# One VectorE maximum over four score banks in place of four maxima, in a fused attention and SwiGLU kernel

## The chip, the cores and the metric

The kernel runs on one core of one Trainium2 chip. The metric is the device time of one execution in microseconds, as the median of several runs.

## The reference

Eight batches of eight heads attend over 576 positions with a head width of 64. Scores that lie more than `tau` under the largest of their row are dropped before the softmax. The result is laid out as 4608 tokens of 512 features and goes through a SwiGLU block of width 1536. Everything is float32.

```python
scores = scale * np.matmul(q, k.transpose(0, 1, 3, 2))          # (8, 8, 576, 576), scale = 1/8
thresh = np.max(scores, axis=-1, keepdims=True) - tau
scores = np.where(scores >= thresh, scores, -1000000000.0)
scores = scores - np.max(scores, axis=-1, keepdims=True)
attn = np.exp(scores)
attn = attn / (np.sum(attn, axis=-1, keepdims=True) + 1e-09)
attn_out = np.matmul(attn, v)
x = attn_out.transpose(0, 2, 1, 3).reshape(4608, 512)
g = x @ w_gate
out = (g / (1 + np.exp(-g)) * (x @ w_val)) @ w_out
```

## The kernel before

A unit of attention work is a pair of heads of one batch, so there are 32 pairs. The program has three stages.

**Early tiles (7 to 130 us).** The four pairs of the first batch go through `scores()`, 20 query tiles in all. A tile of 128 rows puts the scores of its two heads into two PSUM tiles `sc` of two banks each; the last 64 rows of a pair need one such tile. VectorE takes one maximum per PSUM tile (L455), ScalarE the exponentials (L459), VectorE masks and sums them (L462).

**Main slots (130 to 1143 us).** The other 28 pairs take three slots each, 84 in all, and twelve slots make up one batch. `slot_scores` (L1705) runs 32 small score products (64 PE instructions) into two PSUM tiles, one per head, of two banks. Bank 0 and bank 1 of a head hold 288 columns each of units u=0 and u=1, and behind them 144 columns each of unit u=2. Then `slot_rest` lists the work on the other engines:

- four maxima on VectorE, two for each head: units 0 and 1 in one instruction (L1726), unit 2 in the other (L1728). They write six columns of `mx`, negated;
- a query row's keys lie in two groups of 32 partitions, so the six values are exchanged between neighbouring groups, by VectorE (`largest`, four instructions, L1734) or by ScalarE (`others`, four copies, L1740), and one small reduce joins own and other value into `nm` (L1735 or L1744);
- ScalarE makes the threshold `th` from `nm` (L1747);
- for each of the six (head, unit) blocks ScalarE writes the exponential of the scores (L1751, "E" in what follows), and VectorE multiplies it by the comparison of the scores with the threshold and sums (L1753, "M"). Both read the scores in PSUM;
- ScalarE exchanges the sums (L1761), VectorE adds them and takes the reciprocal (L1766, L1767), ScalarE or POOL scale the blocks (L1779, L1776), VectorE transposes them (L1781). `attend` (L1802) multiplies with the values one pair later.

Between the score products of one slot and the next, TensorE runs products of the SwiGLU block (`block_part`; L993, L1473, L1482, L1269).

**Tail (1143 us on).** The SwiGLU products of the last tokens. `more_banks` hands the score banks to them.

The order on each engine is made by a planner, `Plan`, as the program is written: `job(engine, cost, fn, *deps)` enters a step with an assumed cost, and the planner issues steps by their due times and ranks. TensorE's order is fixed by the code; `slot_scores` waits in the plan for all six M of the slot before (`sc_users`).

What really waits for what on the chip are semaphore waits that the tile framework adds. For a PSUM tile it keeps accesses of different engines in the order in which they were issued, over the whole tile and reads included. In the built program of before, the third E of a slot (head 0, unit 1, bank 1) so waits for the first M of the slot (head 0, unit 0, bank 0), and the first M of head 1 waits only for the first E of head 1, which is in the other tile.

Of the kernel before, what the change touches and what calls it, by code (L numbers as in the profile page):

```python
# [10 lines left out]
F32 = mybir.dt.float32  # L11
# [3 lines left out]
ALU = mybir.AluOpType  # L15
AX = mybir.AxisListType
# [11 lines left out]
class Plan:  # L28
# [12 lines left out]
    def job(self, eng, took, fn, *deps, rank=1, lag=0.0, moves=0.0):  # L41
        j = Job(eng, took, fn, rank, lag, moves)
        for d in deps:
            if isinstance(d, Job) and d.end is None:
                d.then.append(j)
                j.waits += 1
            elif d is not None:
                j.ready = max(j.ready, self.after(d, eng) if isinstance(d, Job) else d + self.HOP)
        if not j.waits:
            self.open[eng].append(j)  # L50
        return j
# [61 lines left out]
def kernel(  # L113
# [11 lines left out]
    nc = tc.nc  # L125
    P = 128
# [5 lines left out]
    G = 32  # L132
# [7 lines left out]
    SH = S // 2  # L140
    NU3 = 3
    SQ = SH // 2
# [10 lines left out]
    const = ctx.enter_context(tc.tile_pool(name="const", bufs=1))  # L153
    qkp = ctx.enter_context(tc.tile_pool(name="qkp", bufs=2))
    stp = ctx.enter_context(tc.tile_pool(name="stp", bufs=4))
    ps_s = ctx.enter_context(tc.tile_pool(name="ps_s", bufs=2, space=bass.MemoryType.PSUM))
    ps_f = ctx.enter_context(tc.tile_pool(name="ps_f", bufs=1, space=bass.MemoryType.PSUM))
    hbm = ctx.enter_context(tc.tile_pool(name="hbm", bufs=1, space=bass.MemoryType.DRAM))
    ctx.enter_context(tc.manual_schedule())
# [6 lines left out]
    sums = deque(const.tile([P, 2 * NU3, 3], F32, name=f"sums{i}") for i in range(4))  # L166
    for x in sums:
        nc.vector.memset(x[:, :, 2], 1e-9)
    minus2 = const.tile([P, 1], F32, name="minus2")
    nc.vector.memset(minus2, -2.0)  # L170
    junk = const.tile([P, 1], F32, name="junk")
# [249 lines left out]
    heads = [slice(h * D, (h + 1) * D) for h in range(2)]  # L421
# [2 lines left out]
        return TA <= t < NT  # L424

    def statistics(*names):
        return [stp.tile([P, 2 * NU3, 2] if x == "mx" else [P, 2 * NU3], F32, name=x) for x in names]

    def scores(seg, t):
        qT, kT = seg["qT"], seg["kT"]  # L430
        q0 = t * P - seg["q0"]
        if t < NT:
            pss = [ps_s.tile([P, 2, 512], F32, name="sc") for _ in range(2)]
            for h, hs in enumerate(heads):
                cut_ = D if turned(t) and h == 1 else 0
                for n, lo, to in [(0, 0, D), (0, D, SH), (1, 0, SH)] if cut_ else [(0, 0, SH), (1, 0, SH)]:
                    at_ = (n * SH + lo - cut_) % S
                    nc.tensor.matmul(pss[h][:, n, lo:to], qT[hs, q0:q0 + P], kT[hs, at_:at_ + to - lo],
                                     start=True, stop=True)
        else:  # L440
            pss = [ps_s.tile([P, 2, 512], F32, name="sc")]
            for n, h in ((0, 0), (1, 1), (1, 0), (0, 1)):
                hs = heads[h]
                nc.tensor.matmul(pss[0][hs, n, 0:SH], qT[hs, q0:q0 + D], kT[hs, n * SH:(n + 1) * SH],
                                 start=True, stop=True)
        nm, th, ri, tot = statistics("nm", "th", "ri", "tot")
        sm = sums[0]
        sums.rotate(1)
        m = len(pss)
        scs = [ps[:, :, 0:SH] for ps in pss]  # L450
        both = pbufs[0].rearrange("p h s -> p (h s)")[:, KM:KM + P]
        ps = [pbufs[0][:, x, :].rearrange("p (n s) -> p n s", n=2) for x in range(m)]
        pbufs.rotate(1)
        for x in range(m):
            nc.vector.tensor_reduce(out=nm[:, x:x + 1], in_=scs[x], axis=AX.XY, op=ALU.max, negate=True)  # L455
        yield
        for x in range(m):
            nc.scalar.activation(th[:, x:x + 1], nm[:, x:x + 1], AF.Identity, bias=cut, scale=-1.0)
            nc.scalar.activation(ps[x], scs[x], AF.Exp, bias=nm[:, x:x + 1])  # L459
        yield  # L460
        for x in range(m):
            nc.vector.scalar_tensor_tensor(out=ps[x], in0=scs[x], scalar=th[:, x:x + 1], in1=ps[x],  # L462
                                           op0=ALU.is_ge, op1=ALU.mult, accum_out=sm[:, x, 0:1])
        nc.vector.tensor_reduce(out=tot[:, 0:m], in_=sm[:, 0:m, 0:3:2], axis=AX.X, op=ALU.add)
        nc.vector.reciprocal(out=ri[:, 0:m], in_=tot[:, 0:m])
        units = [ident] * m
        if t >= TA:
            for x in range(m):
                if x % 2:
                    nc.gpsimd.tensor_scalar(out=ps[x], in0=ps[x], scalar1=ri[:, x:x + 1], scalar2=None, op0=ALU.mult)  # L470
                else:
                    nc.scalar.activation(ps[x], ps[x], AF.Copy, scale=ri[:, x:x + 1])
        yield
        if t < TA:
            units = [dbufs[0][:, x, :] for x in range(m)]
            dbufs.rotate(1)
            for x in range(m):
                nc.scalar.activation(units[x], ident, AF.Copy, scale=ri[:, x:x + 1])
        unflipped.append((seg, t, both, [(p.rearrange("p n s -> p (n s)"), unit) for p, unit in zip(ps, units)]))
        yield  # L480
# [297 lines left out]
    job, pe = plan.job, plan.pe  # L778
# [113 lines left out]
    stores, summed_g, parts = {}, {}, []  # L892
# [796 lines left out]
    def slot_scores(seg, t):  # L1689


        plan.force(*seg["qk"])
        qT, kT = seg["qT"], seg["kT"]
        deps, sc_users[:] = sc_users[:], []
        pss = []

        def fn():
            pss.extend(ps_s.tile([P, 2, 512], F32, name="sc") for _ in heads)
            for u, part, keys in ((0, (0, slice(0, SH)), (0, SH)), (1, (1, slice(0, SH)), (0, SH)),
                                  (2, (0, slice(SH, SH + SQ)), (0, SQ)), (2, (1, slice(SH, SH + SQ)), (SQ, SH))):  # L1700
                for g in range(NG):
                    a, c = divmod(g, 2)
                    for h, hs in enumerate(heads):
                        col = (NU3 * t + u) * D + a * G
                        nc.tensor.matmul(pss[h][(slice(g * G, (g + 1) * G), *part)], qT[hs, col:col + G],  # L1705
                                         kT[hs, c * SH + keys[0]:c * SH + keys[1]], start=True, stop=True)

        return pss, pe(1.85, fn, *deps, *seg["qk"])

    def slot_rest(seg, t, pss, mark, pooled, max_by_act, rank):  # L1710
        m = 2 * NU3
        mx, nm, th, ri, tot = statistics("mx", "nm", "th", "ri", "tot")
        sm = sums[0]
        sums.rotate(1)
        old_sums, sum_users[0] = sum_users[0], []
# [4 lines left out]
        flat = {x: pall[:, at_of(*x):at_of(*x) + SH] for x in tiles}  # L1720
        ps = {x: y if x[1] < 2 else y.rearrange("p (a n) -> p a n", a=2) for x, y in flat.items()}
        n_of = lambda h, u: NU3 * h + u
        rs = []
        for h, tile_ in enumerate(pss):
            n = n_of(h, 0)
            rs.append(job("DVE", 0.72, lambda n=n, tile_=tile_: nc.vector.tensor_reduce(  # L1726
                out=mx[:, n:n + 2, 0], in_=tile_[:, :, 0:SH], axis=AX.X, op=ALU.max, negate=True), mark, rank=0))
            rs.append(job("DVE", 0.42, lambda n=n, tile_=tile_: nc.vector.tensor_reduce(  # L1728
                out=mx[:, n + 2:n + 3, 0], in_=tile_[:, :, SH:SH + SQ], axis=AX.XY, op=ALU.max, negate=True), mark, rank=0))

        def largest():
            for g in range(NG):
                o = g ^ 1
                nc.vector.tensor_reduce(out=mx[g * G:(g + 1) * G, 0:m, 1], in_=mx[o * G:(o + 1) * G, 0:m, 0:1], axis=AX.X, op=ALU.max)  # L1734
            nc.vector.tensor_reduce(out=nm[:, 0:m], in_=mx[:, 0:m, :], axis=AX.X, op=ALU.min)  # L1735

        def others():
            for g in range(NG):
                o = g ^ 1
                nc.scalar.copy(mx[g * G:(g + 1) * G, 0:m, 1], mx[o * G:(o + 1) * G, 0:m, 0])  # L1740

        if max_by_act:
            oj = job("ACT", 0.78, others, *rs, rank=0)
            nj = job("DVE", 0.18, lambda: nc.vector.tensor_reduce(out=nm[:, 0:m], in_=mx[:, 0:m, :], axis=AX.X, op=ALU.min), oj, rank=0)  # L1744
        else:
            nj = job("DVE", 0.82, largest, *rs, rank=0)
        ej = job("ACT", 0.25, lambda: nc.scalar.activation(th[:, 0:m], nm[:, 0:m], AF.Identity, bias=cut, scale=-1.0), nj, rank=0)  # L1747
        masks = {}
        for h, u in tiles:
            x, n = (h, u), n_of(h, u)  # L1750
# [20 lines left out]
        for u in range(NU3):  # L1771
            scaled = []
            for h in range(2):
                x, n = flat[h, u], n_of(h, u)
# [179 lines left out]
    for s, (n, x) in enumerate((n, x) for n in range(len(halved)) for x in range(NU3)):  # L1954
        seg = halved[n]
        i, t = seg["i"], seg["tiles"][x]
# [43 lines left out]
    def more_banks():  # L2000
        plan.force(*sc_users)
        for _ in range(2):
            ps = ps_s.tile([P, 2, 512], F32, name="sc")
            for h in range(2):
                b_ = Bank(None, ps[:, h])
                banks.append(b_)
# [57 lines left out]
```

## Time and profile before

| | |
|---|---|
| median of 3 runs | 1373.08 us (1371.66 to 1374.05) |
| profiled execution, first to last instruction (span) | 1369.2 us |
| TensorE matmul busy | 1351.0 us, 99% |
| VectorE busy | 1070.9 us, 78% |
| ScalarE busy | 875.5 us, 64% |
| granted TensorE clock | 1.000 |
| the four maxima of the slots, L1726 and L1728 | 124.8 us and 74.8 us, 168 instructions each |

The profiled execution has no other time of its own than its span of 1369.2 us. It is 3.9 us under the median of the runs; these 3.9 us lie around the instructions and are carried along unchanged. Mean durations are of instructions that may overlap by some hundredths of a microsecond with their neighbours on the same engine.

### The profile page before, as it was taken

The numbers are of one execution on the slowest core, as the hardware profiler recorded it, in microseconds if no ns is written. First come the engines' busy times: TensorE is split into PE (matmuls) and PEld (weight loads), VectorE is DVE, ScalarE is ACT, GpSimd is POOL, SyncE is SP. The second block draws the span as 40 slices with busy tenths as digits, with TensorE's granted clock in tenths as the row PEclk, the third lists the DMA queues.
The fourth block names the chain that finished last, engine by engine and source line by source line (L and its number), as shares of the span: only waits on it lengthen the run. The fifth ranks groups of instructions, "written<-read, shape, count | busy, mean of one in ns | idle before, by whom it ended". The sixth has DMA issues, their size and how long they took to land.

```text
span 1369.2 us, 39187 instructions
## 1 busy us (share of the span) xinstructions
PE 1351.0 (99%) x15590; PEld 1116.1 (82%) x15590; DVE 1070.9 (78%) x2815; ACT 875.5 (64%) x2277; POOL 719.9 (53%) x665
## 2 busy tenths in 40 slices
PE   8999999999999999999999999999999999999998
PEld 7777787778788788877887888877887788999998
DVE  7878888887887777777778777777777776787786
ACT  6888776666756766677776766776767764330330
POOL 2688598663564669434973387427943593000000
PEclk9999999999999999999999999999999999999999
DMA  8752424545525540654154513553165403524411
GB/s 177 200 185 90 82 60 133 146 121 156 151 52 155 144 98 27 181 159 117 37 171 128 150 36 128 144 144 87 36 192 144 113 19 143 162 78 146 151 66 32
DMA packets 208294, 162.32 MB, mean 119 GB/s; under 512 B 166128, under 2 KB 180464, under 8 KB 202736
## 3 DMA queue, kind: packets, MB, share of 16 engines
q1 hardware_dynamic: 203920, 158.86, 41.3%
q8 instruction: 124, 2.03, 0.6%
q10 hardware_dynamic: 4192, 0.95, 0.3%
q14 instruction: 58, 0.48, 0.1%
HBM read 138.28 MB, written 21.50 MB: 117 GB/s over the span
## 4 chain that ended last, share of the span: by engine, by line
PE 90%; DVE 3%; DMA 2%; POOL 2%; SPq 1%; issue 1%; ACT 1%; ACTq 0%; DVEq 0%; POOLq 0%
PE pb L993 18%; PE pa L993 12%; PE px L1473 12%; PE sc L1705 10%; PE pe L993 9%; PE xa L1802 9%; PE po L1269 5%; PE py L1482 5%; PE sc L1154 2%; PE pg L1200 2%; PE pv L1200 2%; PE pe L1154 1%; SPq L367 1%; DMA wo<-in_moe_w_val_dram 1%; PE sc L1473 1%
## 5 line engine op out<-in xcount | busy, mean ns | idle before, releaser
L1753 DVE SCALAR_TENSOR_TENSOR pall<-sc,th,pall 128x288 f32<-128x288 f32 x504 | 244.0, 514 | 65.1 <-ACT pall L1751 50.7
L993 PE MATMUL pb<-xall,big 128*128 128x256 f32 x1152 | 273.5, 380 | 0.0
L1751 ACT ACTIVATE pall<-sc,nm 128x288 f32<-128x288 f32 x504 | 232.2, 498 | 34.1 <-DVE pall L1753 33.8
L993 PEld LDWEIGHTS pb<-xall,big 128*128 128x128 f32 x1152 | 216.4, 190 | 31.0 <-issue 2.2
L1781 DVE STREAM_TRANSPOSE pall<-pall 128x576 f32<-128x576 f32 x252 | 189.7, 765 | 58.2 <-ACT pall L1779 41.4
L1779 ACT ACTIVATE pall<-pall,ri 128x288 f32<-128x288 f32 x415 | 189.8, 529 | 26.3 <-DVE ri L1767 25.8
L846 POOL TENSOR_TENSOR hall<-hall,tmp 128x512 f32<-128x512 f32 x80 | 102.3, 1279 | 159.3 <-DVE hall L1046 141.9
L993 PE MATMUL pa<-xall,big 128*128 128x256 f32 x768 | 183.4, 382 | 0.0
L993 PEld LDWEIGHTS pa<-xall,big 128*128 128x128 f32 x768 | 143.0, 190 | 22.2 <-issue 2.7
L1705 PE MATMUL sc<-kT,qT 64*32 64x144 f32 (+1 forms) x5376 | 150.0, 345 | 2.9 <-DVE pall L1753 1.7
L1726 DVE TENSOR_REDUCE mx<-sc 128x2 f32<-128x576 f32 x168 | 124.8, 743 | 28.6 <-PE sc L1705 28.1
L1705 PEld LDWEIGHTS sc<-kT,qT 64*32 64x32 f32 x5376 | 97.8, 106 | 56.9 <-issue 21.0
L993 PE MATMUL pe<-xall,big 128*128 128x256 f32 x576 | 137.2, 381 | 0.4 <-issue 0.4
L1802 PE MATMUL xa<-pall,vall 64*32 64x288 f32 x4032 | 133.0, 404 | 0.9 <-DVE hall L1046 0.8
L1776 POOL TENSOR_SCALAR pall<-pall,ri 128x288 f32<-128x288 f32 x89 | 88.9, 1010 | 67.0 <-DVE ri L1767 63.8
L993 PEld LDWEIGHTS pe<-xall,big 128*128 128x128 f32 x576 | 108.5, 190 | 17.3 <-issue 2.8
L1802 PEld LDWEIGHTS xa<-pall,vall 64*32 64x32 f32 x4032 | 76.5, 107 | 50.6 <-issue 7.4
L1761 ACT COPY sums<-sums 32x6 f32<-32x6 f32 x336 | 66.8, 199 | 45.6 <-DVE pall L1753 41.1
L1045 ACT ACTIVATE vall<-tmp 128x512 f32<-128x512 f32 x96 | 60.2, 630 | 24.6 <-DVE tmp L1058 9.0
L1482 PE MATMUL py<-wo,hall 128*128 128x256 f32 x336 | 74.8, 379 | 0.0
L1728 DVE TENSOR_REDUCE mx<-sc 128x1 f32<-128x288 f32 x168 | 74.8, 445 | 0.0
L846 POOL TENSOR_TENSOR tmp<-tmp 128x512 f32<-128x512 f32 x36 | 45.9, 1276 | 53.4 <-ACT tmp L1068 53.4
(258 smaller groups left out, 2481.3 us busy)
## 6 DMA issues: line engine op xcount, KB each, us to landing
big<-sums_hbm SPq DMA_DIRECT2D x42, 1024.0 KB, 5.4
big<-sums_hbm SPq DMA_DIRECT2D x48, 768.0 KB, 4.7
vall<-in_v_dram SPq DMA_DIRECT2D x112, 144.0 KB, 3.0
out_dram<-big SPq DMA_DIRECT2D x32, 256.0 KB, 3.0
qT<-in_q_dram SPq DMA_DIRECT2D x112, 72.0 KB, 4.8
kT<-in_k_dram SPq DMA_DIRECT2D x112, 72.0 KB, 3.0
wo<-in_moe_w_gate_dram SPq DMA_DIRECT2D x16, 384.0 KB, 4.1
wo<-in_moe_w_val_dram SPq DMA_DIRECT2D x16, 384.0 KB, 4.8
```

Source lines behind the costliest of these rows:

```text
L846: return lambda: nc.gpsimd.tensor_tensor(out=out, in0=a, in1=b, op=op)
L993: nc.tensor.matmul(ps[:, i], w[:, k_, i * P:(i + 1) * P], x[:, k_, :], start=first and i == k_ == 0, stop=True, skip_group_check=True)
L1473: nc.tensor.matmul(ps, a[:, f, :], ws[n][:, f, :], start=bank_ not in begun, stop=True, skip_group_check=True)
L1482: nc.tensor.matmul(ps(), a[:, f, i * P:(i + 1) * P], operands[o][:, f, :], start=first and f == 0, stop=True, skip_group_check=True)
L1705: nc.tensor.matmul(pss[h][(slice(g * G, (g + 1) * G), *part)], qT[hs, col:col + G], kT[hs, c * SH + keys[0]:c * SH + keys[1]], start=True, ...
L1726: rs.append(job("DVE", 0.72, lambda n=n, tile_=tile_: nc.vector.tensor_reduce(out=mx[:, n:n + 2, 0], in_=tile_[:, :, 0:SH], axis=AX.X, op= ...
L1751: ej = job("ACT", 0.42, lambda x=x, n=n: nc.scalar.activation(ps[x], scs[x], AF.Exp, bias=nm[:, n:n + 1]), ej, *((masks[h, 0], masks[h, 1] ...
L1753: masks[x] = job("DVE", 0.45, lambda x=x, n=n: nc.vector.scalar_tensor_tensor(out=ps[x], in0=scs[x], scalar=th[:, n:n + 1], in1=ps[x], op0 ...
L1776: scaled.append(job("POOL", 1.02, lambda x=x, n=n: nc.gpsimd.tensor_scalar(out=x, in0=x, scalar1=ri[:, n:n + 1], scalar2=None, op0=ALU.mul ...
L1779: scaled.append(job("ACT", 0.46, lambda x=x, n=n: nc.scalar.activation(x, x, AF.Copy, scale=ri[:, n:n + 1]), rj, rank=rank))
L1781: seg["turned"].append(job("DVE", 0.72, lambda both=both: nc.vector.transpose(out=both, in_=both), *scaled, rank=rank))
L1802: nc.tensor.matmul(holds[a].ap()[x * G:(x + 1) * G, 0:SH].rearrange("d (i q) -> d i q", q=G), vr[rs, h, j, ds], p[rs, h, :, j, :], start=( ...
```

## The change

The two score tiles of two banks become one tile `sc_all` of four banks, allocated once. The slots, the early tiles (`scores`) and `more_banks` take halves of it where they took tiles. In a slot, one VectorE reduce reads all four banks, 432 columns of each in three parts of 144, and leaves twelve partial maxima. The exchange moves twelve columns in place of six. Two small reduces (`least`) join them into the six values of `nm`: one for units 0 and 1 (each in two parts, own and other), one for unit 2 (one part in each of two banks, own and other). `mx` comes from two fixed buffers in place of the pool `stp`. The planner's assumed costs change with it: 1.95 for the one reduce (before 0.72 and 0.42, twice), 0.98 for `largest` (0.82), 0.34 for `least` (0.18).

```diff
-    ps_s = ctx.enter_context(tc.tile_pool(name="ps_s", bufs=2, space=bass.MemoryType.PSUM))
+    ps_s = ctx.enter_context(tc.tile_pool(name="ps_s", bufs=1, space=bass.MemoryType.PSUM))
...
+    maxima = deque(const.tile([P, 4 * NU3, 2], F32, name=f"mx{i}") for i in range(2))
...
+    sc_all = ps_s.tile([P, 4, 512], F32, name="sc")
+    halves = deque(sc_all[:, 2 * h:2 * h + 2] for h in range(2))
+
+    def next_half():
+        halves.rotate(-1)
+        return halves[-1]
...
-            pss = [ps_s.tile([P, 2, 512], F32, name="sc") for _ in range(2)]
+            pss = [next_half() for _ in range(2)]
...
-            pss.extend(ps_s.tile([P, 2, 512], F32, name="sc") for _ in heads)
+            pss.extend(sc_all[:, 2 * h:2 * h + 2] for h in range(2))
...
-        rs = []
-        for h, tile_ in enumerate(pss):
-            n = n_of(h, 0)
-            rs.append(job("DVE", 0.72, lambda n=n, tile_=tile_: nc.vector.tensor_reduce(
-                out=mx[:, n:n + 2, 0], in_=tile_[:, :, 0:SH], axis=AX.X, op=ALU.max, negate=True), mark, rank=0))
-            rs.append(job("DVE", 0.42, lambda n=n, tile_=tile_: nc.vector.tensor_reduce(
-                out=mx[:, n + 2:n + 3, 0], in_=tile_[:, :, SH:SH + SQ], axis=AX.XY, op=ALU.max, negate=True), mark, rank=0))
+        parts = sc_all[:, :, 0:SH + SQ].rearrange("p b (s k) -> p b s k", k=SQ)
+        rs = [job("DVE", 1.95, lambda: nc.vector.tensor_reduce(
+            out=mx.rearrange("p (b s) o -> p b s o", s=NU3)[:, :, :, 0], in_=parts, axis=AX.X, op=ALU.max, negate=True), mark, rank=0)]
+        both_parts = mx.rearrange("p (h b s) o -> p h b (s o)", h=2, b=2)
+        nm_of = nm.rearrange("p (h u) -> p h u", h=2)
+
+        def least():
+            nc.vector.tensor_reduce(out=nm_of[:, :, 0:2], in_=both_parts[:, :, :, 0:4], axis=AX.X, op=ALU.min)
+            nc.vector.tensor_reduce(out=nm_of[:, :, 2], in_=both_parts[:, :, :, 4:6], axis=AX.XY, op=ALU.min)
...
-            nc.vector.tensor_reduce(out=nm[:, 0:m], in_=mx[:, 0:m, :], axis=AX.X, op=ALU.min)
+            least()
```

More of the change, by code (lines that the diff above doesn't have):

```diff
@@ L426, in statistics @@
     def statistics(*names):
-        return [stp.tile([P, 2 * NU3, 2] if x == "mx" else [P, 2 * NU3], F32, name=x) for x in names]
+        return [stp.tile([P, 2 * NU3], F32, name=x) for x in names]
+    sc_all = ps_s.tile([P, 4, 512], F32, name="sc")
[3 more added lines that the diff above has]
+        return halves[-1]
     def scores(seg, t):
@@ L440, in scores @@
         else:
-            pss = [ps_s.tile([P, 2, 512], F32, name="sc")]
+            pss = [next_half()]
             for n, h in ((0, 0), (1, 1), (1, 0), (0, 1)):
@@ L1711, in slot_rest @@
         m = 2 * NU3
-        mx, nm, th, ri, tot = statistics("mx", "nm", "th", "ri", "tot")
+        nm, th, ri, tot = statistics("nm", "th", "ri", "tot")
+        mx = maxima[0]
+        maxima.rotate(1)
         sm = sums[0]
@@ L1733, in largest @@
                 o = g ^ 1
-                nc.vector.tensor_reduce(out=mx[g * G:(g + 1) * G, 0:m, 1], in_=mx[o * G:(o + 1) * G, 0:m, 0:1], axis=AX.X, op=ALU.max)
-            nc.vector.tensor_reduce(out=nm[:, 0:m], in_=mx[:, 0:m, :], axis=AX.X, op=ALU.min)
+                nc.vector.tensor_reduce(out=mx[g * G:(g + 1) * G, :, 1], in_=mx[o * G:(o + 1) * G, :, 0:1], axis=AX.X, op=ALU.max)
+            least()
         def others():
@@ L1739, in others @@
                 o = g ^ 1
-                nc.scalar.copy(mx[g * G:(g + 1) * G, 0:m, 1], mx[o * G:(o + 1) * G, 0:m, 0])
+                nc.scalar.copy(mx[g * G:(g + 1) * G, :, 1], mx[o * G:(o + 1) * G, :, 0])
         if max_by_act:
             oj = job("ACT", 0.78, others, *rs, rank=0)
-            nj = job("DVE", 0.18, lambda: nc.vector.tensor_reduce(out=nm[:, 0:m], in_=mx[:, 0:m, :], axis=AX.X, op=ALU.min), oj, rank=0)
+            nj = job("DVE", 0.34, least, oj, rank=0)
         else:
-            nj = job("DVE", 0.82, largest, *rs, rank=0)
+            nj = job("DVE", 0.98, largest, *rs, rank=0)
         ej = job("ACT", 0.25, lambda: nc.scalar.activation(th[:, 0:m], nm[:, 0:m], AF.Identity, bias=cut, scale=-1.0), nj, rank=0)
@@ L2002, in more_banks @@
         for _ in range(2):
-            ps = ps_s.tile([P, 2, 512], F32, name="sc")
+            ps = next_half()
             for h in range(2):
```

## The prediction

> **What bounds the kernel now.** I read the page first: engines, the chain that ended last, then the groups of the slot's lines.
>
> ```profile
> span 1369.2 us, 39187 instructions
> PE 1351.0 (99%) x15590; PEld 1116.1 (82%) x15590; DVE 1070.9 (78%) x2815; ACT 875.5 (64%) x2277; POOL 719.9 (53%) x665
> PE 90%; DVE 3%; DMA 2%; POOL 2%; SPq 1%; issue 1%; ACT 1%; ACTq 0%; DVEq 0%; POOLq 0%
> L1753 DVE SCALAR_TENSOR_TENSOR pall<-sc,th,pall 128x288 f32<-128x288 f32 x504 | 244.0, 514 | 65.1 <-ACT pall L1751 50.7
> L1751 ACT ACTIVATE pall<-sc,nm 128x288 f32<-128x288 f32 x504 | 232.2, 498 | 34.1 <-DVE pall L1753 33.8
> L1726 DVE TENSOR_REDUCE mx<-sc 128x2 f32<-128x576 f32 x168 | 124.8, 743 | 28.6 <-PE sc L1705 28.1
> L1728 DVE TENSOR_REDUCE mx<-sc 128x1 f32<-128x288 f32 x168 | 74.8, 445 | 0.0
> ```
>
> TensorE is busy for all but 18 us, so VectorE time saved in a slot can give back at most part of 18 us. What can cost more is a slot whose VectorE and ScalarE work no longer fits beside TensorE's. So I next read the timeline of slot 23, whose E and M have nothing else between them (columns: start, us, engine, line, idle before).
>
> ```profile
> 395.54 0.87 ACT L1751 ACTIVATE pall<-sc,nm 128x288 f32<-128x288 f32 x2
> 396.06 0.52 DVE L1753 SCALAR_TENSOR_TENSOR pall<-sc,th,pall 128x288 f32<-128x288 f32 x1
> ...
> 396.50 0.52 DVE L1753 SCALAR_TENSOR_TENSOR pall<-sc,th,pall 128x288 f32<-128x288 f32 x1
> 396.62 0.94 ACT L1751 ACTIVATE pall<-sc,nm 128x288 f32<-128x288 f32 x2 [0.20 <-DVE pall L1753]
> ...
> 397.15 0.52 DVE L1753 SCALAR_TENSOR_TENSOR pall<-sc,th,pall 128x288 f32<-128x288 f32 x1
> ...
> 398.69 0.52 DVE L1753 SCALAR_TENSOR_TENSOR pall<-sc,th,pall 128x288 f32<-128x288 f32 x1
> ```
>
> E of one head runs beside M of the other: the six E and six M take 3.66 us, from 395.54 to 399.20. Each head's own E and M alternate (the third E starts at 396.62, 0.03 after the first M's end), because they share a PSUM tile. That two tiles interleave is what keeps the chain short.
>
> Last, I read from the timeline of all slots how a slot's period is made up. Slots 60 to 71 (848.3 to 995.5 us) repeat three more times. Their mean, in us: score products 1.75, to the first maximum 0.32, four maxima 2.13, exchange and `nm` 1.14, to `th` 0.24, to the first E 0.20, E and M 4.58 (other work stands between), last M to the next score products 1.91: together 12.27.
>
> **The maxima.** Removed are 743+445+743+445 ns a slot, which stand 2.13 us on the clock because neighbours overlap. Both rows fit 0.147 us and 1.035 ns an element (743-445 over 288), so one reduce of 1728 elements is 0.147+1.788 = 1.94. The ends are 1.79 (no fixed part) and 2.13 (nothing saved, if reading four banks in twelve runs costs more). I take 1.94, as both rows are the same instruction: -0.19. The exchange grows from six to twelve columns: 6 elements more in each of four instructions, under 0.03; no row has twelve, so 0 to 0.1, taken 0.02. The second join is like L1735 (0.17 us); overlapping its neighbour it adds 0.09 to 0.17, taken 0.10. Net -0.07 a slot, ends -0.2 to +0.3. VectorE loses 0.44-0.2 us of busy time a slot, which buys nothing by itself, as it is idle for 22%.
>
> The Trainium skill ("VectorE: DVE Perf Modes", the section on the TRN2 errata) says that a large tile pays the fixed latency once where small ones pay each time, which speaks for the change as the fit does. It is not what decides.
>
> **The joined tile.** All scores are now one PSUM tile, and in the built program of after every E and M of a slot wait in the order of issue, across heads. Resolving the waits: in slot 23 it reads EE|M|E|M|E|MM|E|M|E|M, with a wait on the other engine at each bar; before, the two heads' sequences ran side by side. Nothing that overlapped can overlap now. With rows of slot 23 (first two E 0.875, one E 0.50, one M with its accumulator read 0.525, two M 0.965, from an end to a released start 0.034): 0.875+0.525+0.50+0.525+0.50+0.965+0.50+0.525+0.50+0.515+9x0.034 = 6.24 against 3.66. The 84 sequences differ little (5 to 9 bars); summed in the same way, with the work that stands between E and M laid into the gaps, they give 5.9 to 6.9, mean 6.21. Before, the mean from first E to last M was 4.41. Growth 1.80 a slot, 1.60 in the repeating part; less the 0.07 it is 1.73.
>
> The rule against this change is the skill's "PSUM — Partial Sum Buffer", section on bank collisions: engines must be kept apart by bank and 32-partition quadrant, two reads included. By it E of bank 1 beside M of bank 0 is free, the chain stays near 3.7 and the time near 1372. The rows of before already show a coarser order: the third E reads bank 1 and still waits for M on bank 0 of its tile. So I go by the waits.
>
> **What hides it.** Queued behind the waiting E on ScalarE are the copies of SwiGLU products and the sum exchange; behind the waiting M on VectorE the transposes; and TensorE's next score products wait for the last M. TensorE's slack is the 1.91 (0.6 to 3.8 by slot) less a 0.16 release. But the slack is not free each time: VectorE and ScalarE owe the rest of the slot before they can begin the next. Slot 64, whose last M ends at 905.88:
>
> ```profile
> 905.93 0.83 ACT L1761 COPY sums<-sums 32x6 f32<-32x6 f32 x4 [0.86 <-DVE pall L1753]
> ...
> 907.48 2.67 ACT L1779 ACTIVATE pall<-pall,ri 128x288 f32<-128x288 f32 x6
> ...
> 908.48 0.78 DVE L1781 STREAM_TRANSPOSE pall<-pall 128x576 f32<-128x576 f32 x1 [1.28 <-ACT pall L1779]
> 909.18 0.72 DVE L1726 TENSOR_REDUCE mx<-sc 128x2 f32<-128x576 f32 x1
> ```
>
> The next maximum starts 3.3 us after the last M, through exchange, sums, scaling and one transpose, though the score products were there at 908.41. Over slots 60 to 71 this route, with its waits on TensorE taken out, is 1.95 to 5.3, mean 3.64. So a slot that waits only for itself takes 3.64+1.94+(1.14+0.12)+0.24+0.20+6.18 = 13.46 against 12.27: 1.19 more, and TensorE waits for it. By the other count: growth 1.73 less VectorE's mean wait for score products before the first maximum, 0.34, which is all the air in the loop: 1.39 over all 84 slots, where the first 36 grow more (4.21 to 6.25). 84 x 1.39 = 117.
>
> **Early tiles and the rest.** There `scores` has E, E, then M, M. Both reduces now precede the first E (0.66 later), the first M follows the second E (0.8 later), and the next score products, which start 0.16 after the first M in most tiles (10 of 20 start 0.5 to 0.7 before the last M's end), wait for the last. I take 1.2 us for each of 16 two-head tiles, less 4.2 of slack after the ninth and about 0.9 at each of four single-head ones that only one buffer hid: 19-4-4 = 11, from 3 to 20. TensorE's order is unchanged, instruction by instruction. On SP two transfers of SwiGLU sums (one store, one load) stand some places later, and on POOL some twenty instructions swap with neighbours; POOL is at 53% and these are not waited for soon: 0, or 2 us if one is. The tail's waits on score banks are the same. Its 0 holds as long as TensorE's order does.
>
> Sum: 1369.2+117+11 = 1497 for the profiled execution, 1501 with the 3.9 around it.
>
> The skill's "TensorE: Matmul & The Clock Gate" (Part 1) halves the clock after about 3.4 us of idleness. The rows show 1.00 throughout, with gaps up to 1.8 us; stalls of 1 to 3 us would stay under it.
>
> **Rivals.** *TensorE's slack counts anew each slot.* If VectorE and ScalarE catch up, only max(0, growth - slack) is lost: 4.5 us per twelve repeating slots, 46 in all, with 8 early: 1427. For it: VectorE is idle 22%; against it: slot 64 above. *Nothing is absorbed.* 84 x 1.73 = 145 and 20 early: 1538; for it are the slots where the next maximum starts without VectorE having idled (46 of 84). *Not slower.* E and M wait for other things anyway: if the work between them already spaces them so that the chain from first E to last M grows by less than the 0.07 saved, the gain is at most some 2 us, in slots 1, 4 and 7 where the score products start before the last M ends: 1371. Against it, only 10 of 84 slots now exceed 5.3, and the shortest sequence of after is 5.8. It decides if that chain stays under 4.5. That the change doesn't do what it says is excluded: the built program has the one reduce.
>
> **How the numbers follow.** Forecast 0.64, slack anew 0.19, nothing absorbed 0.13, not slower 0.04. The range, 1425 to 1540, takes in most of the first three. A difference under 0.2% can't be told from none here: faster 0.02, same 0.02, slower 0.96.
>
> **What would show it.** E and M of one slot must no longer overlap, and first E to last M be about 6.2; the reduce 1.94; TensorE's idle time at the score products grow from 2.9 us to about 110, released by the last M; its busy time stay at 1351. A chain near 4.5 would prove the waits harmless; a chain of 6.2 with under 60 us lost would prove the slack rival.

## The result and the profile after

After the change the kernel takes 1490.67 us (median of 5 runs, 1485.69 to 1491.18), beside 1373.08 us (median of 5 runs, 1371.66 to 1374.77) for the kernel before: a ratio of 1.0852 (1.0839 to 1.0865). The forecast was 1501 us. The profiled execution of after took 1490.66 us, its span is 1488.9 us, which is 119.7 more than the 1369.2 of before.

From the page of after, the same parts as were shown of before: the engines, the chain that ended last, and the groups (busy us, mean ns of one | idle time before it and what ended most of it).

```profile
span 1488.9 us, 38913 instructions
PE 1373.7 (92%) x15590; PEld 1123.8 (75%) x15590; DVE 1068.7 (72%) x2647; ACT 881.5 (59%) x2277; POOL 718.5 (48%) x665
DVE 33%; PE 32%; ACT 23%; issue 6%; POOL 4%; DMA 2%; SPq 0%; ACTq 0%; DVEq 0%; POOLq 0%
L1765 DVE SCALAR_TENSOR_TENSOR pall<-sc,th,pall 128x288 f32<-128x288 f32 x504 | 249.3, 517 | 192.9 <-ACT pall L1763 190.8
L1763 ACT ACTIVATE pall<-sc,nm 128x288 f32<-128x288 f32 x504 | 234.3, 496 | 156.8 <-DVE pall L1765 154.3
L1001 PE MATMUL pb<-xall,big 128*128 128x256 f32 x1152 | 281.0, 387 | 21.3 <-ACT tmp L1045 17.1
L1713 PE MATMUL sc<-kT,qT 64*32 64x288 f32 (+1 forms) x5376 | 157.7, 359 | 58.1 <-DVE pall L1765 57.3
L1734 DVE TENSOR_REDUCE mx<-sc 128x12 f32<-128x1728 f32 x84 | 162.2, 1930 | 13.7 <-PE sc L1713 13.4
```

No engine is busier than before by more than TensorE's 22.7 us, and yet the chain that ended last went from 90% TensorE to a third on each of VectorE and TensorE and a quarter on ScalarE: the bound is now a loop through three engines, none of which is full. E (L1763) and M (L1765) take as long as before, 496 and 517 ns. What has changed is the time before them: M waits 190.8 us for E (50.7 before) and E 154.3 us for M (33.8 before).

The timeline of slot 23 shows how (start, us, engine, line, and in brackets the idle time before and its releaser).

```profile
445.68 0.88 ACT L1763 ACTIVATE pall<-sc,nm 128x288 f32<-128x288 f32 x2
446.59 0.52 DVE L1765 SCALAR_TENSOR_TENSOR pall<-sc,th,pall 128x288 f32<-128x288 f32 x1 [0.49 <-ACT pall L1763]
...
447.15 0.50 ACT L1763 ACTIVATE pall<-sc,nm 128x288 f32<-128x288 f32 x1 [0.59 <-DVE pall L1765]
447.69 0.52 DVE L1765 SCALAR_TENSOR_TENSOR pall<-sc,th,pall 128x288 f32<-128x288 f32 x1 [0.57 <-ACT pall L1763]
...
451.47 0.52 DVE L1765 SCALAR_TENSOR_TENSOR pall<-sc,th,pall 128x288 f32<-128x288 f32 x1 [0.57 <-ACT pall L1763]
```

Each line begins where one on the other engine has just ended. From the first E to the end of the last M it is 451.99-445.68 = 6.31 us, where before it was 3.66. Over all slots the stages stand so (mean us a slot, worked out from the records of all E, M, reduces and score products; the two last columns are means of the 83 steps from a slot to the next; "E beside M" is the time that E and M of a slot run at once; the stretch from `nm` to the first E, which has no column, is 0.43 before and 0.36 after):

| | reduce | to `nm` | first E to last M | E beside M | last M to next maximum | period |
|---|---|---|---|---|---|---|
| before | 2.13 | 1.15 | 4.41 | 1.45 | 3.93 | 12.05 |
| after | 1.93 | 1.24 | 6.11 | 0.00 | 3.74 | 13.36 |

By stage of the program: slot 0's score products start at 139.5 us, 8.8 later than before; from there to the start of slot 83 it is 1109.2 us, 109.3 more; the rest takes 1.6 more. 8.8+109.3+1.6 = 119.7.

### The profile page after: what moved, and what is told of

Read it like the earlier page. It is cut to its first block, busy times and chain, and to the rows that moved or that the text cites. A ratio compares the mean times of both kernels' runs of the same rounds, so it can differ in the third digit from the quotient of the medians.

```text
span 1488.9 us, 38913 instructions
## 1 busy us (share of the span) xinstructions
PE 1373.7 (92%) x15590; PEld 1123.8 (75%) x15590; DVE 1068.7 (72%) x2647; ACT 881.5 (59%) x2277; POOL 718.5 (48%) x665
## 4 chain that ended last, share of the span: by engine, by line
DVE 33%; PE 32%; ACT 23%; issue 6%; POOL 4%; DMA 2%; SPq 0%; ACTq 0%; DVEq 0%; POOLq 0%
DVE pall L1765 13%; ACT pall L1763 12%; PE pb L1001 8%; DVE mx L1734 7%; PE px L1481 5%; DVE pall L1793 4%; PE sc L1713 4%; PE pa L1001 4%; PE xa L1814 3%; ACT pall L1791 2%; POOL pall L1788 2%; ACT sums L1773 2%; PE sc L1162 2%; PE py L1490 1%; DVE mx L1746 1%
## 5 line engine op out<-in xcount | busy, mean ns | idle before, releaser
L1765 DVE SCALAR_TENSOR_TENSOR pall<-sc,th,pall 128x288 f32<-128x288 f32 x504 | 249.3, 517 | 192.9 <-ACT pall L1763 190.8
L1763 ACT ACTIVATE pall<-sc,nm 128x288 f32<-128x288 f32 x504 | 234.3, 496 | 156.8 <-DVE pall L1765 154.3
L1001 PE MATMUL pb<-xall,big 128*128 128x256 f32 x1152 | 281.0, 387 | 21.3 <-ACT tmp L1045 17.1
L1713 PE MATMUL sc<-kT,qT 64*32 64x288 f32 (+1 forms) x5376 | 157.7, 359 | 58.1 <-DVE pall L1765 57.3
L1791 ACT ACTIVATE pall<-pall,ri 128x288 f32<-128x288 f32 x415 | 189.3, 526 | 23.3 <-DVE ri L1779 22.7
L854 POOL TENSOR_TENSOR hall<-hall,tmp 128x512 f32<-128x512 f32 x80 | 102.1, 1276 | 198.8 <-DVE hall L1054 153.5
L1713 PEld LDWEIGHTS sc<-kT,qT 64*32 64x32 f32 x5376 | 103.0, 109 | 119.0 <-DVE pall L1765 75.8
L1734 DVE TENSOR_REDUCE mx<-sc 128x12 f32<-128x1728 f32 x84 | 162.2, 1930 | 13.7 <-PE sc L1713 13.4
L1814 PEld LDWEIGHTS xa<-pall,vall 64*32 64x32 f32 x4032 | 82.3, 107 | 49.9 <-issue 9.5
L1490 PEld LDWEIGHTS py<-wo,hall 128*128 128x128 f32 x336 | 62.8, 190 | 8.0
```

What stands on the lines that cost most here:

```text
L854: return lambda: nc.gpsimd.tensor_tensor(out=out, in0=a, in1=b, op=op)
L1001: nc.tensor.matmul(ps[:, i], w[:, k_, i * P:(i + 1) * P], x[:, k_, :], start=first and i == k_ == 0, stop=True, skip_group_check=True)
L1490: nc.tensor.matmul(ps(), a[:, f, i * P:(i + 1) * P], operands[o][:, f, :], start=first and f == 0, stop=True, skip_group_check=True)
L1734: rs = [job("DVE", 1.95, lambda: nc.vector.tensor_reduce(out=mx.rearrange("p (b s) o -> p b s o", s=NU3)[:, :, :, 0], in_=parts, axis=AX.X ...
L1763: ej = job("ACT", 0.42, lambda x=x, n=n: nc.scalar.activation(ps[x], scs[x], AF.Exp, bias=nm[:, n:n + 1]), ej, *((masks[h, 0], masks[h, 1] ...
L1765: masks[x] = job("DVE", 0.45, lambda x=x, n=n: nc.vector.scalar_tensor_tensor(out=ps[x], in0=scs[x], scalar=th[:, n:n + 1], in1=ps[x], op0 ...
```

## Experiments

The theory: the joined tile puts every E and every M of a slot into one order, the slot's loop through VectorE and ScalarE becomes longer than TensorE's work, and the time is the loop's. The rivals: the long reduce and the twelve maxima cost it; TensorE's wait for the last M costs it, with slack that counts anew in each slot.

**Which half of the change: e1 and e2.** e1 keeps after's joined tile and has before's four maxima and single join on it; e2 keeps before's two tiles and has after's kind of reduce on each, with twelve partial maxima and after's joins.

```diff
 e1, against after
+        for h, tile_ in enumerate(pss):                     # halves of sc_all
+            ... tensor_reduce(out=mx[:, n:n + 2, 0], in_=tile_[:, :, 0:SH], axis=AX.X, ...)
+            ... tensor_reduce(out=mx[:, n + 2:n + 3, 0], in_=tile_[:, :, SH:SH + SQ], axis=AX.XY, ...)
 e2, against before
+        for h, tile_ in enumerate(pss):                     # two tiles
+            ... tensor_reduce(out=mx.rearrange("p (b s) o -> p b s o", s=NU3)[:, 2 * h:2 * h + 2, :, 0],
+                in_=tile_[:, :, 0:SH + SQ].rearrange("p b (s k) -> p b s k", k=SQ), axis=AX.X, ...)
```

Expected of e1:

> One part alone: the joined tile of four banks, with the four maxima and the single join of before. If the waits of the joined tile are the cause, E and M of a slot still don't overlap, first E to last M is about 6.1 us, and the time is that of the full change plus some 0.1 us a slot for the four maxima (2.13 for 1.93 us, a join shorter by 0.1): 1498 us, between 1485 and 1505. If instead the one long reduce and its longer join delay the slot (rival), the time is back at 1373.

Expected of e2:

> The other part alone: the two tiles of before, one reduce for each head over its two banks in parts of 144 (864 elements, 1.04 us by the rows of before), and the twelve partial maxima with exchange and two joins as in the change. If the joined tile's waits are the cause: first E to last M near 4.4 us again, and 1373 us, between 1369 and 1378. If long reduces and the longer join are the cause (rival), part of the loss stays: over 1400.

e1 took 1488.95 us, ratio 1.0863 (1.0837 to 1.0890): all of the loss. e2 took 1370.16 us, ratio 0.9992 (0.9980 to 1.0004): nothing. So the tile alone costs the time, and four maxima or one on it make no difference that can be measured. e1 keeps the planner's assumed costs of before, too, so the changed costs are not needed for the loss. In e2 each reduce of 864 elements took 1041 ns, and E and M overlap for 1.51 us a slot as before.

**Does TensorE's wait for the tile hold the time? e3 and e6.** In e3 M leaves the scores alone: it compares the exponential with exp(-tau), so that it reads and writes SBUF only, and E no longer has to wait for it.

```diff
 e3, against after
-                out=ps[x], in0=scs[x], scalar=th[:, n:n + 1], in1=ps[x], op0=ALU.is_ge, op1=ALU.mult, accum_out=sm[:, n, 0:1]),
+                out=ps[x], in0=ps[x], scalar=cutp, in1=ps[x], op0=ALU.is_ge, op1=ALU.mult, accum_out=sm[:, n, 0:1]),
+    nc.scalar.activation(cutp, cut, AF.Exp)
 e6, against e3
-                ... in1=ps[x] ...
+                ... in1=other[x] ...       # a constant block of another SBUF tile
```

> The full change, but M compares the exponential in SBUF with exp(-tau), in place of the score in PSUM with the threshold: no M reads the joined tile, so no E waits for an M, and the next score products wait for the last E. The one long reduce and its joins stay. If the waits are the cause: E runs through, first E to last M is 3.6 to 4.5 us, and the time is 1355 to 1380. If the long reduce is (rival): it stays near 1490.

e3 took 1451.55 us, ratio 1.0579 (1.0549 to 1.0609), against an expected 1355 to 1380: a miss. The waits did go; what came in their place is in the groups of e3's page:

```profile
L1767 DVE SCALAR_TENSOR_TENSOR pall<-pall,cutp 128x288 f32<-128x288 f32 x504 | 392.4, 824 | 33.2 <-ACT pall L1765 30.3
L1765 ACT ACTIVATE pall<-sc,nm 128x288 f32<-128x288 f32 x504 | 216.1, 506 | 0.0
L1715 PE MATMUL sc<-kT,qT 64*32 64x144 f32 (+1 forms) x5376 | 148.2, 346 | 2.1 <-ACT pall L1765 1.9
```

E waits for nothing, E and M run at once for 2.12 us a slot, and TensorE stands only 2.1 us at the score products (58.1 in after). But an M takes 824 ns in place of 517, so that six of them take 4.94 of the 5.82 us from first E to last M. So time of this size can be lost with next to no wait of TensorE for the score tile; what that wait is worth in after, e3 does not tell, as its M are longer.

e6 asked whether the 824 ns come from reading one block twice.

> As e3_mask_from_sbuf (full change, M reads no PSUM), but the second operand of M is a constant block of another SBUF tile in place of the exponentials themselves (the masked values are then the comparison times this block). In e3 an M took 824 ns, not 514. If that comes from reading the same block twice, M is near 514 again, first E to last M 3.6 to 4.5, and with one tile and the one long reduce kept the time is 1355 to 1385: the waits alone were the cause. If two SBUF operands cost it, M stays near 820 and the time near 1451.

M again took 824 ns (1452.74 us, ratio 1.0585, 1.0540 to 1.0631), so that is not it. The answer was in e3's own timeline: VectorE and POOL from 408.4 us on.

```profile
408.44 2.32 POOL L856 TENSOR_TENSOR xall<-xall 128x256 f32<-128x256 f32 x3
409.21 0.96 DVE L1767 SCALAR_TENSOR_TENSOR pall<-pall,cutp 128x288 f32<-128x288 f32 x1
...
410.10 0.97 DVE L1767 SCALAR_TENSOR_TENSOR pall<-pall,cutp 128x288 f32<-128x288 f32 x1
410.73 2.74 POOL L856 TENSOR_TENSOR hall<-hall,big 128x256 f32<-128x256 f32 x3
...
412.81 0.97 DVE L1767 SCALAR_TENSOR_TENSOR pall<-pall,cutp 128x288 f32<-128x288 f32 x1
...
413.71 0.51 DVE L1767 SCALAR_TENSOR_TENSOR pall<-pall,cutp 128x288 f32<-128x288 f32 x1
```

Five masks beside POOL's sums take 0.96 to 0.97 us, the sixth, after POOL's end at 413.47, 0.51. Over all 504: the 209 with POOL idle beside them took 509 ns in the mean, the 146 with POOL busy throughout 1171. In after, where one operand comes from PSUM, both kinds took 517. The next runs act on this.

**Is it the order of E and M, and nothing else? e8, e9 and e10.** e8 is e3 with POOL's two-operand arithmetic cut to a few columns; e9 and e10 make the same cut in after and in before.

```diff
     def pool_tt(out, a, b, op):
-        return lambda: nc.gpsimd.tensor_tensor(out=out, in0=a, in1=b, op=op)
+        def run():
+            if out is not a and out is not b:
+                nc.gpsimd.memset(out, 0.0)
+            nc.gpsimd.tensor_tensor(out=few(out), in0=few(a), in1=few(b), op=op)      # 16 columns
+        return run
```

> As e3 (M reads the exponential in SBUF twice and a constant), and POOL's two-operand sums and products (`pool_tt`) work on 16 columns a row only; where the result goes to another place, POOL first fills it with zeros, which reads nothing. So most of POOL's arithmetic is left out; all instructions that it waits for, and that wait for it, stay. In e3's trace the 209 masks beside which POOL stood idle took 509 ns and the 146 beside which it was busy throughout 1171. Theory (POOL's reads lengthen a mask with two SBUF operands, and with a short mask the joined tile costs nothing in the main slots): M falls to 510 to 560 ns, E and M overlap as in e3, first E to last M falls to 4.2 to 4.7, the slot to 12.0 to 12.3, and the time to 1370 to 1395: before's 1373 and some 9 for the early tiles, which this edit doesn't touch. Rival (two SBUF operands lengthen the mask by themselves): M stays over 750 ns and the time over 1435.

> Control for e8: the kernel after, M reading the scores in PSUM as it does there, with the same cut of POOL's arithmetic. If the wait of E and M on each other holds the time, and not POOL, nearly all of the loss stays: 1470 to 1492, M at 515 ns, first E to last M at 6.1. If POOL's length is part of the loop (its scaling ends sooner, transposes wait for it 24 us), up to 25 us less than after: 1465. If POOL held the time in e3 and after alike, under 1420.

> Control: the kernel before with the same cut of POOL's arithmetic. TensorE is busy for 99% of the span there and its order stays: 1366 to 1375. Under 1360 would say that POOL was part of what bounds before, and then e8 can't be compared with before.

From e8's page:

```profile
span 1373.3 us, 39175 instructions
PE 90%; DVE 4%; ACT 2%; DMA 1%; SPq 1%; issue 1%; POOL 0%; ACTq 0%; DVEq 0%
L1775 DVE SCALAR_TENSOR_TENSOR pall<-pall,cutp 128x288 f32<-128x288 f32 x504 | 240.8, 523 | 45.2 <-ACT pall L1773 40.6
```

M is back at 523 ns, E and M overlap for 1.83 us a slot, first E to last M is 4.22, the period 11.97, and the chain is TensorE's for 90% again. e8 took 1375.28 us, ratio 1.0009 (0.9998 to 1.0019), with the joined tile, the one reduce and the twelve maxima all in it. e10 took 1371.90 us, ratio 0.9989 (0.9980 to 0.9999): the cut of POOL's arithmetic is worth next to nothing where TensorE is the bound. e9 took 1479.59 us, ratio 1.0770 (1.0752 to 1.0788), with E and M at 6.10 us and no overlap. From e9's page:

```profile
L1773 DVE SCALAR_TENSOR_TENSOR pall<-sc,th,pall 128x288 f32<-128x288 f32 x504 | 249.2, 516 | 192.6 <-ACT pall L1771 190.6
L1771 ACT ACTIVATE pall<-sc,nm 128x288 f32<-128x288 f32 x504 | 233.9, 496 | 156.3 <-DVE pall L1773 153.8
```

e8 and e9, on one chip, differ in what M reads, and by 104 us. Two things follow from what M reads: in e8 E no longer waits for M, and the next score products wait for the last E in place of the last M. The second cannot be much of the loss in after. VectorE waits for score products for 13.4 us there in all (28.1 before), so late products hold up the slots by no more than that; and e7, below, keeps their wait for the last M and is some 86 us faster. So the loss is the order of E and M.

POOL's length is about a tenth of the loss in after (1.0770 against 1.0852, some 11 us). Part of it is seen in the transposes' wait for POOL's scaling, 24.4 us in after and 18.2 in e9; where the rest comes from is not shown.

**Is it a loop? e4, e5 and e7.** e4 leaves the sum exchange out of after, and e5 out of before.

```diff
-        xj = job("ACT", 0.78, exchange, *masks.values(), rank=1)
+        xj = job("ACT", 0.78, lambda: None, *masks.values(), rank=1)
...
-            nc.vector.tensor_reduce(out=tot[:, 0:m], in_=sm[:, 0:m, :], axis=AX.X, op=ALU.add)
+            nc.vector.tensor_reduce(out=tot[:, 0:m], in_=sm[:, 0:m, 0:3:2], axis=AX.X, op=ALU.add)
```

> The full change without the four copies that exchange the sums between partition groups (each row is then divided by the sum over half of its keys; every other instruction stays in its place). They lie after the last M, so not between a slot's score products and the next ones, but on the way from the last M to the next maximum (0.83 of about 3.7 us). If the loop through VectorE and ScalarE sets the period, as forecast, the time falls by 0.6 to 0.8 us in most slots: 1430 us, between 1415 and 1450. If TensorE's slack counts anew in each slot (rival), nothing moves: 1486 to 1492.

> The kernel before without the four copies that exchange the sums (each row is divided by the sum over half of its keys), as a control for the same edit on the full change, which gained 24 us there. If the loop through VectorE and ScalarE is the bound only with the joined tile, TensorE holds the time here and nothing moves: 1368 to 1376. If the copies cost time whatever the bound (rival), some 24 us are gained here too: 1347.

e5 took 1372.27 us, ratio 0.9992 (0.9979 to 1.0004): in before the exchange is off the path. e4 took 1467.14 us, ratio 1.0701 (1.0671 to 1.0730), some 21 to 23 less than after (by the ratios and by the times). The direction is the loop's, the size is not what was expected (1430). In the timeline of after behind slot 64's last M one sees why:

```profile
1003.44 0.77 DVE L1793 STREAM_TRANSPOSE pall<-pall 128x576 f32<-128x576 f32 x1
1003.56 0.83 ACT L1773 COPY sums<-sums 32x6 f32<-32x6 f32 x4 [1.03 <-DVE pall L1765]
...
1003.58 1.72 PE L1713 MATMUL sc<-kT,qT 64*32 64x288 f32 x64 [0.79 <-DVE pall L1765]
...
1004.42 0.17 DVE L1778 TENSOR_REDUCE tot<-sums 128x6 f32<-128x18 f32 x1 [0.21 <-ACT sums L1773]
...
1005.03 2.66 ACT L1791 ACTIVATE pall<-pall,ri 128x288 f32<-128x288 f32 x6
...
1006.73 1.92 DVE L1734 TENSOR_REDUCE mx<-sc 128x12 f32<-128x1728 f32 x1
```

The exchange runs for 0.83 us beside a transpose of 0.77 that VectorE does in any case; only 0.21 of it is waited for. The score products that waited for the last M end at 1005.30, and the maximum starts at 1006.73: it is the route through VectorE and ScalarE that it waits for. Over all slots e4's stretch from the last M to the next maximum is 0.28 shorter (3.46 against 3.74), and its period 0.26 (13.11 against 13.36): 83x0.26 = 21 us. The saving is that of the route, slot by slot, with next to nothing absorbed.

e7 keeps after and lists the six E ahead of the six M, so that one wait stands where there were nine in slot 23, still without overlap.

```diff
-            ej = job("ACT", 0.42, lambda x=x, n=n: nc.scalar.activation(...), ej, *((masks[h, 0], masks[h, 1]) if u == 2 else ()), rank=0)
+            ej = job("ACT", 0.42, lambda x=x, n=n: nc.scalar.activation(...), ej, rank=0)
+        for h, u in tiles:
+            x, n = (h, u), n_of(h, u)
             masks[x] = job("DVE", 0.45, ...
```

> The full change with the six E of a slot listed ahead of the six M, so that the built program has one switch between them in place of five to nine. Nothing overlaps still: six E (2.70) and six M (2.73) with one release are 5.5 us for 6.1. The plan's times change with it, so TensorE's SwiGLU products stand in a somewhat other order. If the chain through the joined tile sets the period: 84 x 0.6 = 50 us less, 1440, between 1420 and 1460. If the long reduce or TensorE's slack were the matter (rivals): 1480 or more.

It took 1404.44 us, ratio 1.0233 (1.0195 to 1.0272), less than the 1420 to 1460 expected. First E to last M fell by only 0.32 (to 5.79), but the stretch behind the last M fell by 0.88, to 2.86: while ScalarE does its six E without a break, VectorE does transposes and sums that otherwise come after the last M (its other work between first E and last M grew from 1.03 to 1.75 us a slot, and behind the last M it fell from 2.40 to 1.49). That second part was not in the expectation. The lines of E and M on e7's page:

```profile
L1766 DVE SCALAR_TENSOR_TENSOR pall<-sc,th,pall 128x288 f32<-128x288 f32 x504 | 227.2, 513 | 76.4 <-ACT pall L1763 75.8
L1763 ACT ACTIVATE pall<-sc,nm 128x288 f32<-128x288 f32 x504 | 213.0, 504 | 0.0
```

The period is 12.31 and TensorE's busy time is 1350.6 us again. E and M overlap for 0.00 us in e7 too, so what after loses is not the overlap as such but the length of the loop; with runs of six more of the slot's other work fits into the long gaps. The plan's order of the SwiGLU products differs a little in e7, and what that is worth was not tried by itself.

No kernel here is faster than before by more than the 0.2% that can be told; e2 and before are the same.

## Why the prediction was right, by its steps

**The bound and the direction.** "VectorE time saved can give back at most part of 18 us" holds: e2 has the saved instructions and shows 0.9992. The loss was read from the waits of the built program, and the sequence EE|M|E|M|E|MM|E|M|E|M stands in slot 23 of after at each place.

**The maxima.** The reduce of 1728 elements: 1.94 forecast, 1.93 measured. To `nm`: 0.12 more forecast, 0.09 measured. The sentence of the skill that the prediction draws on here is about SBUF latency, and the maxima read PSUM; what carried the forecast was the fit to the rows of before.

**First E to last M.** 6.24 forecast for slot 23, 6.31 measured; 6.21 in the mean, 6.11 measured. All 84 slots lie between 5.7 and 7.0 (5.9 to 6.9 forecast). Overlap: none, as said.

**The PSUM rule.** By the skill's "PSUM — Partial Sum Buffer" (bank collisions) engines have to be kept apart by bank and quadrant, by which E beside M of another bank is free; that would have given about 1372. The measurement decides for the coarser order: E of one bank and M of another never overlap in after, and do for 1.45 us a slot with two tiles. The page tells what the memory needs, the tile's waits ask for more.

**The loop.** In the repeating slots 60 to 71: 13.46 forecast, 13.40 measured (3.86 to the maximum, 1.93, 1.21, 0.12, 0.20, 6.08). That it came so close is in part luck: the stretch from the last M to the maximum was 0.22 longer than the 3.64 of the sum, and the other terms together 0.28 shorter. The growth over all slots was 1.39 by forecast and is 1.32 (109.3 over 83 steps), again with terms mis-sized in opposite directions. First E to last M grew by 1.70 instead of 1.80, and `nm` to the first E fell by 0.07 where nothing was forecast; but of the 0.34 that VectorE waited for score products before the maximum only 0.18 was absorbed (0.16 is left, 13.4 us in all), where all of it was to go. 109 us in place of 117.

**Early tiles, tail, and what lies around.** 8.8 in place of 11, and 1.6 in place of 0. Of the 3.9 us around the span half was wrong: after has 1490.66-1488.9 = 1.8 around its span. The spans of before's other runs go from 1367.2 to 1374.0 us with 2.1 to 2.3 us around them, so nearly half of the 3.9 was a profiled execution on the short side. 7.7+2.2-1.6+2.1 = 10.4 us is the whole difference between 1501 and 1490.67.

**Where TensorE would stand idle: wrong.** About 110 us at the score products were forecast, with a busy time of 1351. It was 58.1 at the score products, 25.1 at the SwiGLU products (0.4 before), 21.3 at the first tiles' scores (5.5 before), and the busy time went up by 22.7. The lines of after's waits (us in all, times, longest):

```profile
PE sc L1713 <- DVE pall L1765: 57.3, 39, 4.7
PE pb L1001 <- ACT tmp L1045: 17.1, 11, 2.6
```

The prediction named the copies of the SwiGLU products as queued behind the waiting E on ScalarE, but did not ask who waits for them in turn: TensorE does, for the bank that the copy L1045 empties. This did not move the sum, since the period was counted along VectorE and ScalarE. Nor does TensorE's idle time at one line measure a loss: 58 us there was no proof of the slack rival, as the slots lost 109. In all, TensorE's idle time went from 18.2 to 115.2 us, and these 97.0 with the 22.7 of busy time are the 119.7 of the span.

**The clock: wrong.** "Stalls of 1 to 3 us would stay under it" did not hold, see below. The 34 us at half clock can account for some 17 of the 22.7 us, as an estimate from the granted clock of 0.5. How much of the 22.7 lies on the path was not tried by itself; VectorE's whole remaining wait for score products before the maximum is 13.4 us, 28.1 before, so score products alone don't put much of it there. It stays open for the SwiGLU products.

**The rivals.** Slack anew (1427) falls by the slots' 109 us against 46, and by e4: its four copies stand behind the last M, where the next score products wait for nothing more, and some 21 us went with them. Nothing absorbed (1538) falls by the measured 109 against 145. Not slower falls by first E to last M, which is under 5.7 in no slot.

## What to carry to other kernels

As the waits stand in these built programs, a PSUM tile is a unit of order between engines: before joining tiles to save instructions, look which engines work on different parts of them at the same time, and add up their chain with a wait at each change of engine. An engine busy for 72% can still hold the time, so count the loop along the engines that hand work to each other, and take time off it only where somebody waits for that time. If two engines must alternate on one tile, runs can cost far less than turns: six and six cost 2.3% here, turns 8.5%.

## What was not expected of the hardware

**VectorE's two SBUF operands and POOL.** A mask of 128x288 float32 takes 509 ns with both large operands in SBUF and POOL idle, 1171 ns with POOL busy throughout (727 beside its one-operand work alone, 1278 beside its two-operand work alone), and 517 ns with one operand in PSUM whether POOL is idle or busy. POOL's own two-operand products beside it went from 1276 to 1386 ns. The skill's "GPSIMD Engine Reference" (Key points) states that contention for VectorE instructions with two SBUF inputs; the time with POOL busy, 1171 in place of 509, is its size here. With M back at 523 ns it is most of the 76 us between e3 and e8; the same cut of POOL's work was worth 11 us in after.

**Half clock after short gaps.** In before the granted TensorE clock is 1.00 but for the end. In after nine stretches, one of 6.8 us and eight of 3.4, run at 0.5, about 34 us in all. They begin in gaps of TensorE of 2.26 to 4.71 us or just behind them; four of these gaps were 2.34 to 2.35 us. Other gaps of 1.91 to 2.74 us had none. One of them in TensorE's timeline of after:

```profile
737.40 2.63 PE L1001 MATMUL pb<-xall,big 128*128 128x256 f32 x8 [2.35 <-ACT tmp L1045]
739.97 2.69 PE L1713 MATMUL sc<-kT,qT 64*32 64x288 f32 x64
```

The score products take 2.69 us where they take 1.72 at the full clock; the granted clock from 740 to 743 us is 0.66 in the mean. By the rule of the skill's "TensorE: Matmul & The Clock Gate" (Part 1), about 3.4 us of idleness in a window of its own phase, none of the 2.35 us gaps should have done it; the measurement decides.

The same trace shows what tells the gaps apart. All nine stretches begin on one grid of 3.413 us. In the window of this grid just before each of them TensorE is idle for 1.97 to 3.41 us; of the other windows the most idle one has 1.95. The gap of 2.74 us lies across two windows, which are idle for 1.58 and 1.16. Worked out in the same way for the other runs with such stretches (e1, e3, e4 and e6 to e9), no half-clock stretch begins behind a window with under 1.87 us of idleness, and every window with over 1.95 is followed by half clock. So in these runs it is the idle time within a window that goes with the half clock, and somewhat over half of the window is enough.
